# Attention scores with keys on partitions, exp without maximum behind a branch, denominators by sums and a product with ones

## The chip, the cores and the metric

The kernel runs on one core of one Trainium2 chip. A core has five engines with a queue each: TensorE for matrix products (PE in the profile, PEld for its weight loads), VectorE (DVE), ScalarE (ACT), GpSimd (POOL) and SyncE (SP, which here only issues DMAs). The matrix products here write to PSUM tiles; the other operands lie in SBUF. The metric is the device time of the whole program in microseconds (us); the median of three runs before the change is 2140.26 us (2139.71 to 2141.01).

## The reference

Attention over 8 batches, 12 heads, 448 rows and head dimension 64, with q and k divided by the root of their mean square and multiplied by g, and then a feed-forward with squared relu on the 3584 x 768 result:

```python
def rmsnorm(x, g):
    rms = np.sqrt(np.mean(x * x, axis=-1, keepdims=True) + 1e-06)
    return x / rms * g
q_n, k_n = (rmsnorm(q, g_q), rmsnorm(k, g_k))
scores = (1.0 / np.sqrt(64)) * np.matmul(q_n, k_n.transpose(0, 1, 3, 2))
scores = scores - np.max(scores, axis=-1, keepdims=True)
attn = np.exp(scores)
attn = attn / (np.sum(attn, axis=-1, keepdims=True) + 1e-09)
x = np.matmul(attn, v)         # then (B, H, S, D) -> (B*S, H*D)
h = np.maximum(x @ w_in, 0.0)  # w_in: 768 x 2048
out = h * h @ w_out            # w_out: 2048 x 768
```

The setup draws g_q and g_k as |normal| + 0.5. The weights w_in and w_out come as float64, and the kernel makes float32 numbers of their two words itself; all else is float32.

## The kernel before

A sequence of 448 rows is held as 4 chunks of 112 (NJ = 4, CP = 112): partition p holds rows 4p to 4p + 3. Heads go in pairs, 48 in all, six pairs to a batch. For a pair, `load` brings q, k and v (SP). `normalize` squares q and k (POOL, L93), sums (DVE), takes the power -1/2 (POOL, rr, L100) and multiplies q and k by it (POOL, qkn, L105). `turn` transposes both (PE, tr, L121), so that the even head's 64 dimensions lie on the lower half of the partitions and the odd head's on the upper, and multiplies by g (DVE, L122).

Then a pair has 8 steps, one for each head and chunk of queries. `score` makes 112 x 448 scores with queries on the partitions (PE, sc, L132), their negative maximum (DVE, nmax, L134), exp with the sum of each row (ACT, L137), the reciprocal of the sum and the product with it (DVE, L139 to L141). Two steps later (LAG) `turn_weights` transposes that block in four pieces (PE, trw, L150), and ACT (L153, even head) or DVE (L155, odd head) copies it out of PSUM. `attend` multiplies with v (PE, av, L165): 8 products a pair, the even head writing the lower half of the PSUM tile and the odd head the upper; one copy (DVE, L170) makes a sixth of the batch's xT.

The feed-forward of batch b - 1 is a generator, `ffn`: 16 blocks f of hps (PE, L190, six products each), relu (ACT, L199), squares on POOL (L204, L205, L209, L210), then yps (PE, L219, 16 products for each half of an output tile, 3 tiles for an even batch and 4 for an odd one), copies and stores. Its pieces are placed evenly among the steps of batch b's attention; the last batch's run alone at the end. Only PE's order is written out by hand, by this loop. The other engines' orders are made by a scheduler from priorities and its estimates, and every engine then runs its queue in order.

The weights come in 56 pieces, 24 of w_in (128 x 512) and 32 of w_out (128 x 384), over the first 72 steps (WEIGHT_STEPS), that is 9 pairs. `to_float32` needs for each piece five DVE instructions (L278, L285, L289, L293, L297), three on POOL (L282, L302, L303) and one on ACT (L301), in a chain between the engines. Pieces of w_out pass through two tiles (tag y), those of w_in through eight.

Of the kernel before, what the change touches and what calls it, by code (L numbers as in the profile page):

```python
# [10 lines left out]
F32 = mybir.dt.float32  # L11
U32 = mybir.dt.uint32
# [12 lines left out]
WEIGHT_STEPS = 72  # steps over which the weights are loaded: more than a batch's attention has  # L25
LAG = 2  # steps between a chunk's scores and the transposes of its weights
# [3 lines left out]
def kernel(  # L30
# [10 lines left out]
):  # L41
    nc = tc.nc
# [11 lines left out]
    const = ctx.enter_context(tc.tile_pool(name="const", bufs=1))  # L54
    io = ctx.enter_context(tc.tile_pool(name="io", bufs=3))
# [3 lines left out]
    ps_sc = ctx.enter_context(tc.tile_pool(name="ps_sc", bufs=3, space=bass.MemoryType.PSUM))  # L59
    ps_tr = ctx.enter_context(tc.tile_pool(name="ps_tr", bufs=2, space=bass.MemoryType.PSUM))  # L60
    ps_av = ctx.enter_context(tc.tile_pool(name="ps_av", bufs=1, space=bass.MemoryType.PSUM))
# [3 lines left out]
    gq = const.tile([P, 1], F32, name="gq")  # L65
    gk = const.tile([P, 1], F32, name="gk")
# [5 lines left out]

    pairs = [(b, c) for b in range(B) for c in range(NPAIR)]
    loaded, normal, turned, weights, xts = {}, {}, {}, {}, {}

    def load(i):
        b, c = pairs[i]
        qk = io.tile([CP, 2, 2, NJ, D], F32, name="qk", tag="qk", bufs=2)
        vt = io.tile([CP, 2, NJ, D], F32, name="vt", tag="vt")
        for dst, src in ((qk[:, 0], q), (qk[:, 1], k), (vt, v)):  # L80
            nc.sync.dma_start(
                dst.rearrange("p h j d -> p h (j d)"),
                src[b, 2 * c : 2 * c + 2].rearrange("h (p j) d -> p h (j d)", j=NJ),
            )
        loaded[i] = qk, vt

    def normalize(i):
        """Rows of q and k over their root mean square, the two heads' rows side by side."""
        qk = loaded[i][0]
        qkn = att.tile([CP, 2, NJ, 2, D], F32, name="qkn", tag="qkn", bufs=1)  # L90
        rows = qk.rearrange("p x h j d -> p (x h j) d")
        squares = qkn.rearrange("p x j h d -> p (x j h) d")
        nc.gpsimd.tensor_tensor(out=squares, in0=rows, in1=rows, op=ALU.mult)  # L93
        ms = small.tile([CP, 4 * NJ], F32, name="ms", tag="ms", bufs=2)
        nc.vector.tensor_reduce(out=ms, in_=squares, axis=AX.X, op=ALU.add)
        nc.vector.tensor_scalar(  # L96
            out=ms, in0=ms, scalar1=1.0 / D, scalar2=1e-6, op0=ALU.mult, op1=ALU.add
        )
        rr = small.tile([CP, 2, 2, NJ], F32, name="rr", tag="rr", bufs=2)
        nc.gpsimd.tensor_tensor(  # L100
            out=rr.rearrange("p x h j -> p (x h j)"), in0=ms,
            in1=minus_half.to_broadcast([CP, 4 * NJ]), op=ALU.pow,
        )
        for x in range(2):
            nc.gpsimd.tensor_tensor(  # L105
                out=qkn[:, x].rearrange("p j h d -> p h j d"),
                in0=qk[:, x],
                in1=rr[:, x, :, :, None].to_broadcast([CP, 2, NJ, D]),
                op=ALU.mult,
            )  # L110
        normal[i] = qkn

    def turn(i):
        """q and k with the head dimension on the partitions, times g (and 1/sqrt(D) for q)."""
        qkn = normal.pop(i)
        qT = att.tile([P, S], F32, name="qT", tag="qT")
        kT = att.tile([P, S], F32, name="kT", tag="kT")
        for x, (dst, g, scale) in enumerate(((qT, gq, D**-0.5), (kT, gk, 1.0))):
            tr = ps_tr.tile([P, S], F32, name="tr", tag="tr")
            for j in range(NJ):  # L120
                nc.tensor.transpose(tr[:, ts(j, CP)], qkn[:, x, j].rearrange("p h d -> p (h d)"), ident[:CP, :CP])  # L121
            nc.vector.tensor_scalar(  # L122
                out=dst, in0=tr, scalar1=g, scalar2=scale, op0=ALU.mult, op1=ALU.mult
            )
        turned[i] = qT, kT

    def score(i, e, j):
        """Attention weights of head e, for its queries of chunk j."""
        qT, kT = turned[i]
        r = ds(e * D, D)  # L130
        sc = ps_sc.tile([CP, S], F32, name="sc", tag="sc")
        nc.tensor.matmul(sc, lhsT=qT[r, ts(j, CP)], rhs=kT[r, :], start=True, stop=True)  # L132
        nmax = small.tile([CP, 1], F32, name="nmax", tag="nmax")
        nc.vector.tensor_reduce(out=nmax, in_=sc, axis=AX.X, op=ALU.max, negate=True)  # L134
        w = att.tile([CP, S], F32, name="w", tag="w", bufs=3)
        den = small.tile([CP, 1], F32, name="den", tag="den")
        nc.scalar.activation(w, sc, AF.Exp, bias=nmax, accum_out=den)  # L137
        rden = small.tile([CP, 1], F32, name="rden", tag="rden")
        nc.vector.tensor_scalar(out=den, in0=den, scalar1=1e-9, scalar2=None, op0=ALU.add)  # L139
        nc.vector.reciprocal(out=rden, in_=den)  # L140
        nc.vector.tensor_scalar(out=w, in0=w, scalar1=rden, scalar2=None, op0=ALU.mult)  # L141
        return w

    def turn_weights(i, e, j, w):
        """The weights of a chunk of queries with the keys on the partitions."""
        if (i, e) not in weights:
            weights[i, e] = att.tile([CP, NJ, S], F32, name="wT", tag="wT")
        tr = ps_tr.tile([CP, NJ, CP], F32, name="trw", tag="tr")
        for m in range(NJ):
            nc.tensor.transpose(tr[:, m, :], w[:, ts(m, CP)], ident[:CP, :CP])  # L150
        dst = weights[i, e][:, :, ts(j, CP)]
        if e == 0:
            nc.scalar.copy(dst, tr)  # L153
        else:
            nc.vector.tensor_copy(out=dst, in_=tr)  # L155

    def attend(i):
        b, c = pairs[i]
        vt = loaded.pop(i)[1]
        if c == 0:  # L160
            xts[b] = ffn_p.tile([P, NC, S], F32, name="xT", tag="xT")
        av = ps_av.tile([P, S], F32, name="av", tag="av")
        for m in range(NJ):
            for e in range(2):
                nc.tensor.matmul(  # L165
                    av[ds(e * D, D), :], lhsT=vt[:, e, m, :], rhs=weights[i, e][:, m, :],
                    start=m == 0, stop=m == NJ - 1,
                )
        del weights[i, 0], weights[i, 1], turned[i]
        nc.vector.tensor_copy(out=xts[b][:, c, :], in_=av)  # L170

# [10 lines left out]
    def ffn(b):  # L182
        """Yields after each few matrix products."""
# [3 lines left out]
        for f in range(NF):  # L187
            ps = ps_mm.tile([P, S], F32, name="hps", tag="mm")
            for c in range(NC):
                nc.tensor.matmul(  # L190
                    ps, lhsT=w_in_sb[:, c, ts(f, P)], rhs=xT[:, c, :],
# [40 lines left out]
    def store(b, tt, y):  # L232
        """The tile's rows are columns of two batches, each in runs of its chunks."""
# [10 lines left out]

    def weight_chunks():
        """Pieces of the weights in the order of their use: on chip, and in memory."""
# [8 lines left out]
    def load_weights(dst, rows, col):  # L255
# [4 lines left out]
        # In the place of tiles that the products don't need yet.  # L260
# [45 lines left out]
    for t, g in ((gq, g_q), (gk, g_k)):  # L306
        for e in range(2):
            nc.scalar.dma_start(t[ds(e * D, D), :], g.rearrange("(d one) -> d one", one=1))
    nc.vector.memset(minus_half, -0.5)
    make_identity(nc, ident)  # L310
    load(1)

    steps = 2 * NJ
    waiting = deque()
# [4 lines left out]
    with tc.manual_schedule(engines={PE}):  # L319
        normalize(0)  # L320
        turn(0)
        for i, (b, c) in enumerate(pairs):
            if i + 2 < len(pairs):
                load(i + 2)
# [60 lines left out]
```

## Time and profile before

| | before |
|---|---|
| median of 3 runs | 2140.26 us |
| span of the profiled execution | 2137.4 us |
| PE busy | 2007.0 us (94%) |
| DVE busy | 945.0 us (44%) |
| POOL busy | 646.1 us (30%) |
| ACT busy | 483.3 us (23%) |
| mean granted TensorE clock | 0.951 |

The profiled execution spans 2137.4 us from the first instruction to the last; the runs' median is 2.9 us more. Busy PE is not PE at its peak, since products are pipelined and their records overlap: the cost of a product is read from start to start. In the profile each product of float32 operands has two records, a transpose has one. A line of a group reads: line, engine, operation, out<-in, shapes, count | busy us, mean ns of one | idle time before it and what ended it.

### The profile page before, as it was taken

The numbers are of one execution on the slowest core, as the hardware profiler recorded it, in microseconds if no ns is written. First come the engines' busy times: TensorE is split into PE (matmuls) and PEld (weight loads), VectorE is DVE, ScalarE is ACT, GpSimd is POOL, SyncE is SP. The second block draws the span as 40 slices with busy tenths as digits, with TensorE's granted clock in tenths as the row PEclk, the third lists the DMA queues.
The fourth block names the chain that finished last, engine by engine and source line by source line (L and its number), as shares of the span: only waits on it lengthen the run. The fifth ranks groups of instructions, "written<-read, shape, count | busy, mean of one in ns | idle before, by whom it ended". The sixth has DMA issues, their size and how long they took to land.

```text
span 2137.4 us, 18926 instructions
## 1 busy us (share of the span) xinstructions
PE 2007.0 (94%) x6784; PEld 964.6 (45%) x6784; DVE 945.0 (44%) x2277; ACT 483.3 (23%) x1173; POOL 646.1 (30%) x622
## 2 busy tenths in 40 slices
PE   5567769999999999999999999999999999999999
PEld 2222324455445544454445544454445544455555
DVE  6888786333433344444433344344443344443000
ACT  3222332211221122212221122222222122212100
POOL 6767667211331122221231123221231113210200
PEclk9765659999999999999999999999999999999999
DMA  5311332001000100011000100001000010000000
GB/s 190 91 57 44 92 87 73 13 21 32 14 22 21 32 21 22 17 29 29 17 22 21 29 25 22 18 21 37 18 19 24 21 33 22 9 8 15 0 8 22
DMA packets 47516, 70.42 MB, mean 33 GB/s; under 512 B 4416, under 2 KB 36672, under 8 KB 47424
## 3 DMA queue, kind: packets, MB, share of 16 engines
q1 hardware_dynamic: 47104, 69.22, 11.1%
q8 instruction: 54, 0.88, 0.2%
q14 instruction: 38, 0.31, 0.0%
q10 hardware_dynamic: 320, 0.00, 0.0%
HBM read 58.20 MB, written 11.01 MB: 32 GB/s over the span
## 4 chain that ended last, share of the span: by engine, by line
PE 82%; ACT 1%; issue 0%; DMA 0%; POOL 0%; ACTq 0%
PE yps L219 27%; PE hps L190 27%; PE sc L132 14%; PE trw L150 8%; PE av L165 6%; PE tr L121 1%; ACT wT L153 1%; DMA words<-in_moe_w_out_dram 0%; POOL w_out_sb L303 0%; ACT y L228 0%; POOL words L302 0%; ACT words L301 0%; ACT h L199 0%; ACTq L228 0%; ACTq L301 0%
## 5 line engine op out<-in xcount | busy, mean ns | idle before, releaser
L190 PE MATMUL hps<-xT,w_in_sb 128*128 128x448 f32 x1536 | 609.6, 543 | 0.0
L219 PE MATMUL yps<-w_out_sb,h 128*128 128x384 f32 x1792 | 603.7, 487 | 0.0
L134 DVE TENSOR_REDUCE nmax<-sc 112x1 f32<-112x448 f32 x384 | 238.4, 621 | 660.9 <-PE sc L132 660.9
L132 PE MATMUL sc<-kT,qT 64*112 64x448 f32 x768 | 425.1, 639 | 1.5 <-DVE kT L122 1.5
L219 PEld LDWEIGHTS yps<-w_out_sb,h 128*128 128x128 f32 x1792 | 329.4, 190 | 200.0 <-issue 0.7
L137 ACT ACTIVATE w<-sc,nmax 112x448 f32<-112x448 f32 x384 | 243.9, 635 | 657.5 <-DVE nmax L134 657.3
L190 PEld LDWEIGHTS hps<-xT,w_in_sb 128*128 128x128 f32 x1536 | 281.1, 191 | 228.7 <-issue 228.7
L150 PEld LDWEIGHTS trw<-ident,w 112*112 112x112 f32 x1536 | 156.3, 141 | 348.1 <-issue 244.4
L150 PE MATMUL trw<-ident,w 112*112 112x112 f32 x1536 | 245.0, 286 | 62.3 <-DVE w L141 48.4
L93 POOL TENSOR_TENSOR qkn<-qk 112x1024 f32<-112x1024 f32 x48 | 92.2, 1920 | 519.1 <-issue 424.3
L153 ACT COPY wT<-trw 112x448 f32<-112x448 f32 x192 | 102.1, 532 | 481.8 <-PE trw L150 481.7
L141 DVE TENSOR_SCALAR w<-w,rden 112x448 f32<-112x448 f32 x384 | 204.9, 534 | 9.5
L132 PEld LDWEIGHTS sc<-kT,qT 64*112 64x112 f32 x768 | 111.6, 186 | 201.7 <-issue 193.6
L165 PE MATMUL av<-wT,vt 112*64 112x448 f32 x768 | 175.9, 592 | 22.8 <-DVE wT L155 22.5
L100 POOL TENSOR_TENSOR rr<-ms,minus_half 112x16 f32<-112x16 f32 x48 | 144.7, 3014 | 67.0 <-DVE ms L96 66.9
L209 POOL TENSOR_TENSOR h<-h 128x448 f32<-128x448 f32 x64 | 60.1, 939 | 310.0 <-ACT h L199 310.0
L204 POOL TENSOR_TENSOR h<-h 128x384 f32<-128x384 f32 x64 | 53.2, 831 | 325.8 <-ACT h L199 325.8
L199 ACT ACTIVATE h<-hps 128x448 f32<-128x448 f32 x128 | 69.4, 542 | 306.6 <-PE hps L190 306.6
L139 DVE TENSOR_SCALAR den<-den 112x1 f32<-112x1 f32 x384 | 57.7, 150 | 148.1 <-ACT w L137 148.1
L165 PEld LDWEIGHTS av<-wT,vt 112*64 112x64 f32 x768 | 56.3, 148 | 140.7 <-issue 99.1
L155 DVE COPY wT<-trw 112x448 f32<-112x448 f32 x192 | 117.8, 614 | 2.0 <-PE trw L150 1.8
L105 POOL TENSOR_TENSOR qkn<-qk,rr 112x512 f32<-112x512 f32 x96 | 99.2, 1051 | 3.8
(37 smaller groups left out, 828.5 us busy)
## 6 DMA issues: line engine op xcount, KB each, us to landing
words<-in_moe_w_in_dram SPq DMA_DIRECT2D x24, 512.0 KB, 4.1
words<-in_moe_w_out_dram SPq DMA_DIRECT2D x32, 384.0 KB, 3.1
qk<-in_q_dram SPq DMA_DIRECT2D x48, 224.0 KB, 2.9
qk<-in_k_dram SPq DMA_DIRECT2D x48, 224.0 KB, 3.1
vt<-in_v_dram SPq DMA_DIRECT2D x48, 224.0 KB, 2.7
out_dram<-y SPq DMA_DIRECT2D x8, 336.0 KB, 2.8
out_dram<-y SPq DMA_DIRECT2D x8, 288.0 KB, 2.6
out_dram<-y SPq DMA_DIRECT2D x8, 240.0 KB, 2.7
```

The costliest lines, as they stand in the source:

```text
L100: nc.gpsimd.tensor_tensor(out=rr.rearrange("p x h j -> p (x h j)"), in0=ms, in1=minus_half.to_broadcast([CP, 4 * NJ]), op=ALU.pow,)
L105: nc.gpsimd.tensor_tensor(out=qkn[:, x].rearrange("p j h d -> p h j d"), in0=qk[:, x], in1=rr[:, x, :, :, None].to_broadcast([CP, 2, NJ, D ...
L132: nc.tensor.matmul(sc, lhsT=qT[r, ts(j, CP)], rhs=kT[r, :], start=True, stop=True)
L134: nc.vector.tensor_reduce(out=nmax, in_=sc, axis=AX.X, op=ALU.max, negate=True)
L137: nc.scalar.activation(w, sc, AF.Exp, bias=nmax, accum_out=den)
L141: nc.vector.tensor_scalar(out=w, in0=w, scalar1=rden, scalar2=None, op0=ALU.mult)
L150: nc.tensor.transpose(tr[:, m, :], w[:, ts(m, CP)], ident[:CP, :CP])
L153: nc.scalar.copy(dst, tr)
L155: nc.vector.tensor_copy(out=dst, in_=tr)
L165: nc.tensor.matmul(av[ds(e * D, D), :], lhsT=vt[:, e, m, :], rhs=weights[i, e][:, m, :], start=m == 0, stop=m == NJ - 1,)
L190: nc.tensor.matmul(ps, lhsT=w_in_sb[:, c, ts(f, P)], rhs=xT[:, c, :], start=c == 0, stop=c == NC - 1,)
L219: nc.tensor.matmul(ps, lhsT=h2[f][:, ts(n, P)], rhs=w_out_sb[:, f, ts(half, HALF)], start=f == 0, stop=f == NF - 1,)
```

## The change

The kernel's body becomes a function `program`, called in two arms of a branch. Ahead of it, the elementwise product of g_q and g_k is made on one partition, and its largest magnitude compared with 7.5. Where it is at most that, every score is bounded and the arm `shift=False` runs: exp is taken without subtracting a maximum. The other arm keeps the maximum, with queries on the partitions and transposes.

In the arm without maximum:
- k is not normalized before it is transposed: `turn` transposes raw k, the product of both g's and 1/sqrt(64) goes to q alone, and 1/rms of a key becomes the scale of exp, since keys now lie on the partitions. Only q is multiplied by rr on POOL. The squares move from POOL to ACT (L131). k is loaded in two DMAs, each head's rows 64 numbers at a time, so a load has four DMAs.
- A pair has 4 steps, one for each chunk of keys. `weigh` makes the scores of both heads one behind the other (L184), with 112 keys on the partitions and 448 queries, and exp of both (ACT, L187), which already is what `attend` needs: the 32 transposes trw a pair and their copies are gone, and so are nmax, the sums of rows in exp, and the product with rden (L141).
- `add_up` adds the four chunks of a head on POOL (L201): 6 instructions of 112 x 448 a pair. A product with ones (den, L239, one for each head) sums over the partitions, and lays the result on all 64 partitions of the head. One reciprocal of 128 x 448 (DVE, L249) and one product (DVE, L253) make xT, where a copy stood.
- `attend(i - 1, n)` does one chunk in each step of pair i; den comes in step 1.
- PSUM: four banks for scores and transposes of q and k, two for av and den, two for the feed-forward (before 3, 2, 1 and 2). wT has three buffers for its two heads, xT is six tiles a batch instead of one.
- WEIGHT_STEPS is 36 of 24 a batch, so 9 pairs as before. The feed-forward of batch 0 starts at step 3 of batch 1's 24 (before at step 16 of 48), the later ones at step 4 (before step 2 of 48).

```diff
+    flag = nc.values_load(bounded, min_val=0, max_val=1)
+    with tc.If(flag > 0) as either:
+        program(tc, q, k, v, g_q, g_k, moe_w_in, moe_w_out, out, shift=False)
+    with either.Else():
+        program(tc, q, k, v, g_q, g_k, moe_w_in, moe_w_out, out, shift=True)
...
-        nc.gpsimd.tensor_tensor(out=squares, in0=rows, in1=rows, op=ALU.mult)
+            nc.scalar.activation(squares, qk[:, x], AF.Square)
...
-        for x in range(2):
             nc.gpsimd.tensor_tensor(
-                out=qkn[:, x].rearrange("p j h d -> p h j d"),
+            out=qn.rearrange("p j h d -> p h j d"),
...
+            sc = ps_sc.tile([CP, S], F32, name="sc", tag="sc")
+            nc.tensor.matmul(sc, lhsT=kT[r, ts(m, CP)], rhs=qT[r, :], start=True, stop=True)
+            scs.append(sc)
+        for e, sc in enumerate(scs):
+            nc.scalar.activation(
+                weights[i, e][:, m, :], sc, AF.Exp, scale=normal[i][2][:, 2 * m + e : 2 * m + e + 1]
             )
...
+            so_far = wT[:, 0, :] if m == 1 else sums[i, e]
+            nc.gpsimd.tensor_tensor(out=sums[i, e], in0=so_far, in1=wT[:, m, :], op=ALU.add)
...
-        nc.tensor.matmul(sc, lhsT=qT[r, ts(j, CP)], rhs=kT[r, :], start=True, stop=True)
-        nc.vector.tensor_reduce(out=nmax, in_=sc, axis=AX.X, op=ALU.max, negate=True)
-        nc.scalar.activation(w, sc, AF.Exp, bias=nmax, accum_out=den)
-        nc.vector.tensor_scalar(out=w, in0=w, scalar1=rden, scalar2=None, op0=ALU.mult)
...
+        for e in range(2):
+            nc.tensor.matmul(
+                av[ds(e * D, D), :], lhsT=vt[:, e, m, :], rhs=weights[i, e][:, m, :],
+                start=m == 0, stop=m == NJ - 1,
+            )
+        if m == 1:
+            den = ps_av.tile([P, S], F32, name="den", tag="av")
...
+                nc.vector.reciprocal(out=rden, in_=den)
...
+            nc.vector.tensor_tensor(out=xT, in0=av, in1=normal.pop(i), op=ALU.mult)
...
-                        start = LAG if b > 1 else 2 * steps
+                    start = NJ if b > 1 else WEIGHT_STEPS - NPAIR * NJ - 12
```

How the order on PE changes, in the middle of batch 1's attention, among the hps of batch 0. Before, at a step with attend (trw: transposes of weights, hps: feed-forward):

```order
L190 MATMUL hps<-xT,w_in_sb 128x448 x3
L132 MATMUL sc<-kT,qT 112x448
L165 MATMUL av<-wT,vt 64x448 x8
L150 MATMUL trw<-ident,w 112x112 x4
L190 MATMUL hps<-xT,w_in_sb 128x448 x3
```

Now, in steps 1 and 2 of a pair:

```order
L275 MATMUL hps<-xT,w_in_sb 128x448 x9
L184 MATMUL sc<-qT,kT 112x448 x2
L232 MATMUL av<-wT,vt 64x448 x2
L239 MATMUL den<-sum,ones 64x448 x2
L275 MATMUL hps<-xT,w_in_sb 128x448 x6
L184 MATMUL sc<-qT,kT 112x448 x2
L232 MATMUL av<-wT,vt 64x448 x2
L163 MATMUL tr<-ident,qn 128x112 x4
L163 MATMUL tr<-ident,qk 128x112 x4
```

The eight av of a pair are spread over its steps, both heads' sc stand together, den reads POOL's sums in PE's row, and fewer, larger groups of hps lie between.

POOL's queue, while w_out is made ready. Before, at a pair's normalization (words and w_out_sb: conversion, qkn and rr: normalization):

```order
L100 TENSOR_TENSOR rr<-ms,minus_half 112x16
L105 TENSOR_TENSOR qkn<-qk,rr 112x2x4x64 x2
L302 TENSOR_TENSOR words<-words 128x384
L303 TENSOR_TENSOR w_out_sb<-w_out_sb,words 128x384
L282 TENSOR_SCALAR w_out_sb<-w_out_sb 128x384
```

Now, among batch 0's hps, up to the last sum of pair 7:

```order
L201 TENSOR_TENSOR sum<-sum,wT 112x448
L387 TENSOR_TENSOR words<-words 128x384
L388 TENSOR_TENSOR w_out_sb<-w_out_sb,words 128x384
L367 TENSOR_SCALAR w_out_sb<-w_out_sb 128x384
L201 TENSOR_TENSOR sum<-wT 112x448
L201 TENSOR_TENSOR sum<-sum,wT 112x448
L137 TENSOR_TENSOR rr<-ms,minus_half 112x16
L201 TENSOR_TENSOR sum<-sum,wT 112x448
```

The sums, which PE's den waits for, stand in one queue with the conversion of the weights, 25 of whose 32 pieces of w_out are ahead of the last of these rows.

More of the change, by code (lines that the diff above doesn't have):

```diff
@@ L11 @@
 F32 = mybir.dt.float32
+I32 = mybir.dt.int32
 U32 = mybir.dt.uint32
@@ L144, in turn_weights @@
[L144 to L157, printed above, removed]
-        b, c = pairs[i]
[L159 to L163, printed above, removed]
+                nc.tensor.transpose(tr[:, ts(j, CP)], rows[:, j].rearrange("p h d -> p (h d)"), ident[:CP, :CP])
@@ new lines, in add_up, with weigh_shifted @@
+    def add_up(i, m):
+        if m == 0:
+            return
+        for e in range(2):
+            wT = weights[i, e]
+            if m == 1:
+                sums[i, e] = att.tile([CP, S], F32, name="sum", tag="sum", bufs=2)
+            so_far = wT[:, 0, :] if m == 1 else sums[i, e]
+            nc.gpsimd.tensor_tensor(out=sums[i, e], in0=so_far, in1=wT[:, m, :], op=ALU.add)
+    def weigh_shifted(i, m):
+        qT, kT = turned[i]
+        for e in range(2):
+            r = ds(e * D, D)
+            sc = ps_sc.tile([CP, S], F32, name="sc", tag="sc")
+            nc.tensor.matmul(sc, lhsT=qT[r, ts(m, CP)], rhs=kT[r, :], start=True, stop=True)
+            nmax = small.tile([CP, 1], F32, name="nmax", tag="nmax")
+            nc.vector.tensor_reduce(out=nmax, in_=sc, axis=AX.X, op=ALU.max, negate=True)
+            w = att.tile([CP, S], F32, name="w", tag="w", bufs=1)
+            nc.scalar.activation(w, sc, AF.Exp, bias=nmax)
+            tr = ps_sc.tile([CP, NJ, CP], F32, name="trw", tag="sc")
+            for n in range(NJ):
+                nc.tensor.transpose(tr[:, n, :], w[:, ts(n, CP)], ident[:CP, :CP])
+            nc.vector.tensor_copy(out=weights[i, e][:, :, ts(m, CP)], in_=tr)
+        if m == NJ - 1:
+            for n in range(NJ):
+                add_up(i, n)
@@ L164, in attend @@
             for e in range(2):
                 nc.tensor.matmul(
-                    av[ds(e * D, D), :], lhsT=vt[:, e, m, :], rhs=weights[i, e][:, m, :],
-                    start=m == 0, stop=m == NJ - 1,
-                )
-        del weights[i, 0], weights[i, 1], turned[i]
-        nc.vector.tensor_copy(out=xts[b][:, c, :], in_=av)
+                    den[ds(e * D, D), :], lhsT=ones, rhs=sums.pop((i, e)), start=True, stop=True
+                )
+            rden = att.tile([P, S], F32, name="rden", tag="rden", bufs=1)
@@ new lines, in attend @@
+            if shift:
+                nc.vector.tensor_scalar(
+                    out=rden, in0=den, scalar1=1e-9, scalar2=None, op0=ALU.add
+                )
+                nc.vector.reciprocal(out=rden, in_=rden)
+            else:
+                nc.vector.reciprocal(out=rden, in_=den)
+            normal[i] = rden
+        if m == NJ - 1:
+            xT = ffn_p.tile([P, S], F32, name="xT", tag="xT", bufs=NC + 2)
+            nc.vector.tensor_tensor(out=xT, in0=av, in1=normal.pop(i), op=ALU.mult)
+            xts[b][c] = xT
+            del weights[i, 0], weights[i, 1], turned[i], loaded[i], avs[i]
```

167 lines of the change are left out of this document (102 added, 65 removed).

## The prediction

> **What bounds the kernel now.** I read the page's busy rows and slices first, to find stages.
>
> ```profile
> span 2137.4 us, 18926 instructions
> PE 2007.0 (94%) x6784; PEld 964.6 (45%) x6784; DVE 945.0 (44%) x2277; ACT 483.3 (23%) x1173; POOL 646.1 (30%) x622
> ...
> PE   5567769999999999999999999999999999999999
> ...
> DVE  6888786333433344444433344344443344443000
> ...
> POOL 6767667211331122221231123221231113210200
> PEclk9765659999999999999999999999999999999999
> ```
>
> One slice is 53.4 us. There are two stages. In the first seven slices DVE and POOL are full, PE has holes and is granted 50 to 90% of its clock; afterwards PE is full at 90% or more and nothing else passes half. The windows put numbers on it (columns: time, then busy us and count of PE, PEld, DVE, ACT, POOL, then clock).
>
> ```profile
> 12.00:366.00 354.00, 252.92 (x701) 104.39 (x702) 285.79 (x647) 102.78 (x238) 250.92 (x215) 0.71 0.29 86
> 348.00:1984.00 1636.00, 1623.57 (x5706) 787.00 (x5705) 670.58 (x1655) 373.38 (x926) 391.38 (x387) 1.00 0.08 22
> ```
>
> The chain of work that ended last, asked for in order of time, starts at 342.81 us and is PE from there to the end.
>
> ```profile
> by line: PE yps L219 27.1%; PE hps L190 26.6%; PE sc L132 13.7%; PE trw L150 7.8%; PE av L165 5.9%; PE tr L121 1.1%; ACT wT L153 1.0%; issue 0.4%; DMA words<-in_moe_w_out_dram 0.1%; POOL w_out_sb L303 0.0%; ACT y L228 0.0%; POOL words L302
> ...
> 342.81 3.02 DMA words<-in_moe_w_out_dram
> 348.44 5.77 PE hps L190 x12
> ```
>
> So the second stage is a sum of PE work: products of the feed-forward, (27.1 + 26.6)% of 2137.4 = 1148 us, and attention, (13.7 + 7.8 + 5.9 + 1.1 + 1.0)% = 631 us. At 348 us, 64 steps of 8 a pair are done, so these 631 us are 40 pairs at 15.8 us. The first stage is set by DVE and POOL, which turn the weights into float32 beside the first pairs.
>
> **The change on PE, second stage.** The timeline of PE alone gives the prices (start, us, then what; each product of the program has two records).
>
> ```profile
> 20.39 3.33 PE L132 MATMUL sc<-kT,qT 64*112 64x448 f32 x6 [1.47 <-DVE kT L122]
> ...
> 27.44 1.83 PE L132 MATMUL sc<-kT,qT 64*112 64x448 f32 x2
> ...
> 1222.36 2.76 PE L219 MATMUL yps<-w_out_sb,h 128*128 128x384 f32 x8
> 1225.05 1.00 PE L132 MATMUL sc<-kT,qT 64*112 64x448 f32 x2
> 1225.98 3.23 PE L165 MATMUL av<-wT,vt 112*64 112x448 f32 x16
> 1229.14 0.60 PE L150 MATMUL trw<-ident,w 112*112 112x112 f32 x4
> 1229.58 0.82 PE L219 MATMUL yps<-w_out_sb,h 128*128 128x384 f32 x2
> ```
>
> From start to start, one head's scores hold PE for 1225.98 - 1225.05 = 0.93 us, one chunk's four transposes for 0.44, and eight products of weights and v for 3.16. In the first 30 us, where PE runs slower, one head's scores took 1.83 us and three queued together 3.33: two heads more for 1.50. The even head uses the lower row half and the odd head the upper, so two of the three ran side by side, at the price of one. The 3.16 us are eight times 0.395 for two heads each: they run side by side too.
>
> Per pair the change takes away 32 transposes (8 x 0.44 = 3.5 us) and puts the two heads' scores next to each other: 4 x 0.93 instead of 8 x 0.93, 3.7 us less. It splits weights times v into four couples, 0.79 us each, plus about 0.11 for entering (3.16 less 8 x 0.38 is 0.1), 0.90. It adds two products with ones per pair, a fifth couple beside av, 0.76. The eight transposes of q and k stay, at two chunks' price, 0.87. With 0.09 for going from yps to scores (2.69 from 1222.36 to 1225.05, less 8 x 0.325), a pair costs 4 x (0.09 + 0.93 + 0.90) + 0.76 + 0.87 = 9.3 us against 15.8.
>
> **The first stage.** Two engines share it unequally, and their durations show a coupling (lines of the first window, then of 800 to 1800 us; busy, mean ns).
>
> ```profile
> L141 DVE TENSOR_SCALAR w<-w,rden 112x448 f32<-112x448 f32 x71 | 55.0, 775 | 0.1
> L134 DVE TENSOR_REDUCE nmax<-sc 112x1 f32<-112x448 f32 x71 | 43.1, 609 | 0.8 <-PE sc L132 0.8
> ...
> L134 DVE TENSOR_REDUCE nmax<-sc 112x1 f32<-112x448 f32 x198 | 123.5, 624 | 400.8 <-PE sc L132 400.8
> L141 DVE TENSOR_SCALAR w<-w,rden 112x448 f32<-112x448 f32 x198 | 93.7, 473 | 5.9
> ```
>
> L141, SBUF to SBUF, takes 775 ns where POOL is 71% busy and 473 where it is not; L134, which reads PSUM, takes the same in both. So DVE instructions between SBUF operands wait for POOL. The change removes L141 (55 us), the maxima, the small reciprocals and the copies of transposed weights from DVE, and gives POOL the sums: the load moves to the other side of that coupling. Prices, all of the first window except the last:
>
> ```profile
> 12.00:366.00 354.00, 30.22 (x69) 14.29 (x70) 75.48 (x120) 50.86 (x48) 0.71 0.29 86
> ...
> 12.00:366.00 354.00, 0.00 (x0) 0.00 (x0) 76.45 (x160) 48.82 (x63) 0.71 0.29 86
> ...
> L302 POOL TENSOR_TENSOR words<-words 128x384 f32<-128x384 f32 (+1 forms) x55 | 68.6, 1248 | 76.1 <-issue 30.2 <-ACT wT L153 22.9 <-ACT w L137 17.7
> L100 POOL TENSOR_TENSOR rr<-ms,minus_half 112x16 f32<-112x16 f32 x11 | 37.6, 3417 | 4.0 <-DVE ms L96 3.9
> ...
> L105 POOL TENSOR_TENSOR qkn<-qk,rr 112x512 f32<-112x512 f32 x22 | 23.4, 1083 | 0.9
> ...
> L204 POOL TENSOR_TENSOR h<-h 128x384 f32<-128x384 f32 x3 | 2.5, 820 | 0.0
> L205 POOL TENSOR_TENSOR rest<-h 128x64 f32<-128x64 f32 x3 | 1.0, 327 | 0.0
> ...
> L209 POOL TENSOR_TENSOR h<-h 128x448 f32<-128x448 f32 x64 | 60.1, 939 | 310.0 <-ACT h L199 310.0
> ```
>
> The two window rows are the instructions on w_in_sb and on w_out_sb (PE, PEld, DVE, POOL): all 56 pieces of weights cost DVE 75.5 + 76.5 = 152 us and POOL 50.9 + 48.8 + 68.6 = 168.
>
> PE cannot pass the first product with ones of pair 7 before POOL has ended that pair's sums. In POOL's new order stand ahead of that point: 24 pieces of w_in and 25 of 32 of w_out (50.9 + 25/32 x 48.8 + 49/56 x 68.6 = 149 us), 11 rr (37.6), 10 qn, now of q alone (10.8), 48 sums (at L209's 0.94, the nearest two-operand row of that width: 45.1) and 7 squares of h with their rests (8.0): 250 us. DVE has 75.5 + 25/32 x 76.5 = 135 us of conversion before it, in a chain with POOL's. POOL alone is the lower bound, 250; no overlap at all is the upper, 385. Before, POOL's 251 and the 152 + 55 = 207 us of DVE's SBUF instructions fitted into 354, a ratio of 0.77; 385 x 0.77 = 298. I add 7, since POOL is now the fuller queue and each wait on it counts: 305.
>
> ```profile
> 0.73 0.38 SPq L81 DMA_DIRECT2D qk<-in_q_dram  x1
> ...
> 12.23 0.61 POOL L282 TENSOR_SCALAR w_in_sb<-w_in_sb 128x512 f32<-128x512 f32 x1 [5.80 <-DVE ms L96]
> ...
> gq<-in_g_q_dram ACTq DMA_DIRECT2D x2, 0.2 KB, 3.4
> ```
>
> The branch stands ahead of the first load, now at 0.73 us: the load of g (3.4 us), three small DVE instructions and the flag's way to five engines, which no row shows; between 4 us and 15, I take 7. POOL's first conversion then comes behind two rr and two qn, the second of which waits for qT of pair 0 on DVE; with L100 and L105 twice that is 5 to 6 us more than the 12.23 of now. POOL starts the count at 25, and den of pair 7 can run at 25 + 305 = 330 us.
>
> The Trainium skill ("SBUF — State Buffer", Who interferes with whom) says that GpSimd and VectorE share one pair of ports as an exclusive lock, held for a whole instruction, and that it is taken by VectorE's two-port copies and by its instructions with two SBUF inputs, not by reductions. The two rows of L141 and L134 agree in kind. By that rule as it stands nothing of the 385 overlaps, den of pair 7 runs at 410 and the sum below ends 80 us later; this is a rival below, reckoned from the same rows.
>
> **What lies beside.** ACT gets the squares and kT, and loses half the copies and the reading of sums: 8 x 0.63 + 2 x 0.68 + 0.53 = 7 us a pair of some 33; hidden by PE's products, and in the first stage by POOL. The reciprocal over 448 columns has no row.
>
> ```profile
> L137 ACT ACTIVATE w<-sc,nmax 112x448 f32<-112x448 f32 x71 | 44.9, 632 | 125.0 <-DVE nmax L134 124.8
> ...
> L140 DVE RECIPROCAL rden<-den 112x1 f32<-112x1 f32 x71 | 10.8, 152 | 0.1
> L139 DVE TENSOR_SCALAR den<-den 112x1 f32<-112x1 f32 x71 | 10.1, 143 | 2.9 <-ACT w L137 2.9
> L122 DVE TENSOR_SCALAR qT<-tr,gq 128x448 f32<-128x448 f32 x10 | 6.7, 674 | 3.4 <-PE tr L121 3.4
> ```
>
> Below, it is a plain instruction of that width, 0.67 us; above, each column costs what a whole one-column reciprocal does, 448 x 0.152 = 68 us. One column more than a tensor_scalar costs 9 ns, so I take 0.67 + 448 x 0.009 = 4.7 us. It has two steps, 12 us, before it is needed, and is hidden. The keys' loads in shorter runs and the fourth DMA of a load are asked for two pairs ahead, on SP, behind the weights; hidden, unless SP's wait for a free words tile passes a pair.
>
> **The sum.** When den of pair 7 can run, PE has done 10 of 16 f of the first hps, 60 of 768 products (44 us), and waits there. Left are 1148 - 44 = 1104 us of products and 39.5 pairs x 9.3 = 367. To this come waits: 8 us at den of pair 8, since POOL still has seven pieces (7/32 x 48.8 + 7/56 x 68.6 + five squares + four sums = 29 us, and part of DVE's) against 32 us of PE; 2 us at the head of each of six batches, where five steps without products (11 us of PE) meet 6 x 0.94 + 3.4 + 1.1 = 10.1 us of POOL; 5 us for the last den, reciprocal and xT: 25 us. 330 + 1104 + 367 + 25 = 1826. The profiled execution spans 2137.4 against a median of 2140.26, so 3 us lie around it: 1829, I say 1828, 14.6% less.
>
> **Rivals.**
> - POOL keeps its pace, DVE's waits hide beside it: den of pair 7 free at 275, and then PE sets the point: before hps POOL has 24 + 12 pieces, 10 rr, 9 qn and 42 sums, 197 us, so hps begin near 220, and 44 us of products with six steps of 2.4 end at 280: 1778. For it: POOL was idle 29% of the first window. Against: DVE's 775 ns.
> - The ports exclude each other wholly: 1828 + 80 = 1908. Against: 251 + 207 fitted into 354.
> - PE waits for POOL or ACT in every pair (sums behind a square that waits for relu, scores behind an unread PSUM tile), 2 us x 40: 1908. Against: PE's idle time after 348 us is 12 of 1636 us; but den is a new wait.
> - Couples do not run side by side when they stand alone: 4 x 0.93 more a pair for scores, x 40: 1977. The 3.33 us row speaks against it.
> - Slower: the reciprocal. DVE becomes the bound of the second stage once a pair costs it (2140 - 330)/40 = 45 us; its other work is about 4 us, so from 41 us, 92 ns a column, the kernel is slower; at 152 ns a column it is 330 + 40 x 72 = 3210 us. The 9 ns speak against it.
> - The flag takes the other arm, with maxima and transposes: then PE has 15.8 + 0.76 us a pair: 2140 + 30 = 2170. The reference draws |g| + 0.5 with a fixed seed; the largest product of g_q and g_k there is 5.3, under 7.5, which speaks against it.
>
> **How the numbers follow.** Forecast 0.54, own range 1790 to 1870 (first stage 300 to 360 us, pair 8.9 to 9.8). Faster first stage 0.16, strict ports 0.07, waits in every pair 0.14, no side by side 0.05, reciprocal 0.02, other arm 0.02. The range 1755 to 1900 takes in the forecast, nearly all of the first rival and the lower half of the waits, about 0.8. Runs of this kernel lie within 0.06%; 0.2% is about what can be told from no change. Faster 0.96, same 0.01, slower 0.03.
>
> **What would show it.** In the new profile: scores of two heads starting together, 0.93 us a couple; 9.3 us of attention a pair on PE; POOL over 80% busy until the last w_out piece, near 365 us; den of pair 7 near 330; the reciprocal between 0.7 and 6 us. I am wrong if PE, after the weights are in, idles over 2 us a pair, or if the first stage ends before 300 or after 370.

## The result and the profile after

| | before | after |
|---|---|---|
| median | 2139.99 us (2138.59 to 2141.01) | 1989.33 us (1988.85 to 1992.25) |
| ratio | | 0.930, interval 0.9285 to 0.9311 |
| span of the profiled execution | 2137.4 us | 1987.5 us |
| mean granted TensorE clock | 0.951 | 0.932 |

The kernel became 7.0% faster, 151 us. The forecast was 1828 us with a range of 1755 to 1900: the sign was right, the time lies 89 us above the range. The page of after, its busy rows and the slices of PE, POOL and the clock (one slice is 49.7 us):

```profile
span 1987.5 us, 14446 instructions
PE 1755.0 (88%) x5440; PEld 800.5 (40%) x5440; DVE 496.4 (25%) x602; ACT 423.6 (21%) x741; POOL 823.0 (41%) x814
PE   4446767999999999999999999999999999999998
POOL 6988877433432244423442244423442244411200
PEclk8566688999999989999999999999999999999999
```

The two stages are still there, and the first is no shorter: the chain of work that ended last reaches PE's products at 352 us, before at 348. The surprise is in the second: PE's busy share is lower than before, 88% against 94%, and the clock has a dip in a slice where before all were nines. The windows (time, busy us and count of PE, PEld, DVE, ACT, POOL, then clock, DMA share, GB/s) give the second stage as a whole and the place of a dip:

```profile
351.00:1984.00 1633.00, 1560.28 (x4936) 730.59 (x4936) 243.41 (x259) 330.65 (x575) 542.90 (x550) 0.98 0.08 23
880.00:929.00 49.00, 47.50 (x160) 24.16 (x160) 7.55 (x9) 9.22 (x16) 14.56 (x14) 1.00 0.10 28
929.50:939.00 9.50, 7.66 (x38) 2.53 (x37) 3.46 (x2) 2.91 (x5) 5.86 (x4) 1.00 0.14 41
940.00:950.00 10.00, 8.54 (x18) 2.37 (x18) 2.29 (x4) 4.62 (x8) 5.33 (x5) 0.53 0.21 61
```

PE idles 73 of 1633 us, where before it idled 12 of 1636; and around 940 us, the head of a batch, where five steps stand without products, PE is granted half its clock. No other engine is near full. The groups of PE in that window say at which lines it waits (last columns: idle time before them and what ended it):

```profile
L184 PE MATMUL sc<-qT,kT 64*112 64x448 f32 x628 | 213.0, 614 | 37.4 <-ACT wT L187 33.6 <-ACT kT L169 3.7
L232 PE MATMUL av<-wT,vt 112*64 112x448 f32 x644 | 166.4, 598 | 0.0
L239 PE MATMUL den<-sum,ones 112*64 112x448 f32 x160 | 37.4, 547 | 0.0
L163 PE MATMUL tr<-ident,qk 112*128 112x112 f32 x156 | 23.9, 277 | 37.3 <-DVE qT L165 37.3
```

den, the new wait, costs nothing. The scores wait for exp (ACT L187), and the transposes of k for DVE to read the transposes of q. The timeline of PE at the head of that batch (start, us, instruction, idle before it) shows the sequence:

```profile
934.07 1.01 PE L184 MATMUL sc<-qT,kT 64*112 64x448 f32 x4
935.01 0.97 PE L232 MATMUL av<-wT,vt 112*64 112x448 f32 x4
935.92 0.60 PE L163 MATMUL tr<-ident,qn 112*128 112x112 f32 x4
937.73 0.60 PE L163 MATMUL tr<-ident,qk 112*128 112x112 f32 x4 [1.22 <-DVE qT L165]
938.96 1.00 PE L184 MATMUL sc<-qT,kT 64*112 64x448 f32 x2 [0.62 <-ACT kT L169]
940.68 1.83 PE L184 MATMUL sc<-qT,kT 64*112 64x448 f32 x2 [0.72 <-ACT wT L187]
942.44 1.76 PE L232 MATMUL av<-wT,vt 112*64 112x448 f32 x4
944.98 2.36 PE L184 MATMUL sc<-qT,kT 64*112 64x448 f32 x4 [0.78 <-ACT wT L187]
```

A row "sc x4" is both heads' scores, two records each, side by side; "sc x2" is one head alone. At 934.07 the couple starts together, but in the last step of the pair the even head runs alone at 938.96 and the odd head at 940.68, after the even head's exp. ACT's timeline names what ACT was waiting for:

```profile
940.00 0.63 ACT L187 ACTIVATE wT<-sc,rr 112x448 f32<-112x448 f32 x1 [1.09 <-PE sc L184]
944.29 2.21 ACT L187 ACTIVATE wT<-sc,rr 112x448 f32<-112x448 f32 x4 [2.24 <-PE av L232]
```

At 944.29 four exps run in a row, released by the av of 942.44, the last of the pair before. The table of waits of after (us in total, times, longest) has this in nearly every pair:

```profile
ACT wT L187 <- PE av L232: 94.8, 45, 3.1
PE tr L163 <- DVE qT L165: 91.5, 46, 12.0
PE sc L184 <- ACT wT L187: 50.3, 60, 4.0
```

My reading, which the experiments test: wT has three tiles, each of all four chunks of one head, and a pair needs two. The even head of the next pair gets the third; the odd head's exps must wait until the last av of the pair before has read the whole tile. Until then its scores stay unread in three of the four PSUM banks. The transposes of q and k have to go through the one bank left, one behind the other, and the last couple of scores can't stand together. Of the 152 couples of sc after 400 us, 108 start within 8 ns of each other; 44 stand apart, 38 of them with the odd head at least 1.7 us behind the even one. That is about one of the four couples of a pair.

### The profile page after: what moved, and what is told of

Read it like the earlier page. It is cut to its first block, busy times and chain, and to the rows that moved or that the text cites. A ratio compares the mean times of both kernels' runs of the same rounds, so it can differ in the third digit from the quotient of the medians.

```text
span 1987.5 us, 14446 instructions
## 1 busy us (share of the span) xinstructions
PE 1755.0 (88%) x5440; PEld 800.5 (40%) x5440; DVE 496.4 (25%) x602; ACT 423.6 (21%) x741; POOL 823.0 (41%) x814
## 4 chain that ended last, share of the span: by engine, by line
PE 78%; DVE 3%; ACT 2%; POOL 0%; issue 0%; DMA 0%; ACTq 0%; POOLq 0%
PE yps L304 30%; PE hps L275 27%; PE sc L184 10%; PE av L232 8%; PE tr L163 2%; PE den L239 2%; ACT wT L187 2%; DVE qT L165 1%; DVE rden L249 1%; DMA words<-in_moe_w_out_dram 0%; POOL w_out_sb L388 0%; POOL words L387 0%; ACT kT L169 0%; DVE w_out_sb L370 0%; DVE w_out_sb L374 0%
## 5 line engine op out<-in xcount | busy, mean ns | idle before, releaser
L201 POOL TENSOR_TENSOR sum<-sum,wT 112x448 f32<-112x448 f32 x192 | 220.5, 1148 | 349.3 <-ACT wT L187 342.2
L187 ACT ACTIVATE wT<-sc,rr 112x448 f32<-112x448 f32 x384 | 227.6, 633 | 623.5 <-PE sc L184 528.5
L184 PE MATMUL sc<-qT,kT 64*112 64x448 f32 x768 | 284.6, 657 | 68.8 <-ACT wT L187 50.3
L249 DVE RECIPROCAL rden<-den 128x448 f32<-128x448 f32 x48 | 141.9, 2956 | 476.1 <-PE den L239 476.1
L201 POOL TENSOR_TENSOR sum<-wT 112x448 f32<-112x448 f32 x96 | 110.4, 1150 | 313.7 <-PE den L239 222.5
L232 PE MATMUL av<-wT,vt 112*64 112x448 f32 x768 | 209.5, 628 | 0.0
L184 PEld LDWEIGHTS sc<-qT,kT 64*112 64x112 f32 x768 | 78.8, 191 | 245.1 <-ACT wT L187 116.9
L132 DVE TENSOR_REDUCE ms<-squares 112x8 f32<-112x512 f32 x96 | 65.6, 684 | 203.8 <-ACT squares L131 194.8
L163 PE MATMUL tr<-ident,qk 112*128 112x112 f32 x192 | 32.1, 295 | 91.5 <-DVE qT L165 91.5
L131 ACT ACTIVATE squares<-qk 112x512 f32<-112x512 f32 x96 | 60.3, 628 | 104.0 <-DMA qk<-in_q_dram 49.6
L253 DVE TENSOR_TENSOR xT<-av,rden 128x448 f32<-128x448 f32 x48 | 29.9, 623 | 200.2 <-PE av L232 177.5
```

What stands on the lines that cost most here:

```text
L131: nc.scalar.activation(squares, qk[:, x], AF.Square)
L132: nc.vector.tensor_reduce(out=ms[:, ts(x, 2 * NJ)], in_=squares, axis=AX.X, op=ALU.add)
L163: nc.tensor.transpose(tr[:, ts(j, CP)], rows[:, j].rearrange("p h d -> p (h d)"), ident[:CP, :CP])
L184: nc.tensor.matmul(sc, lhsT=kT[r, ts(m, CP)], rhs=qT[r, :], start=True, stop=True)
L187: nc.scalar.activation(weights[i, e][:, m, :], sc, AF.Exp, scale=normal[i][2][:, 2 * m + e : 2 * m + e + 1])
L201: nc.gpsimd.tensor_tensor(out=sums[i, e], in0=so_far, in1=wT[:, m, :], op=ALU.add)
```

## The experiments

Each kernel was timed in three rounds beside the kernel before, whose median there was 2140.3 to 2141.4 us. Diffs are against after unless they say otherwise; "den of pair 7" is the start of that pair's product with ones, at 324 us in after.

**Chunk tiles.** wT becomes twelve tiles of one chunk instead of three of four chunks: the same bytes.

```diff
-        if m == 0:
-            for e in range(2):
-                weights[i, e] = att.tile([CP, NJ, S], F32, name="wT", tag="wT", bufs=3)
...
+        for e in range(2):
+            weights.setdefault((i, e), []).append(
+                att.tile([CP, S], F32, name="wT", tag="wT", bufs=3 * NJ)
+            )
...
-                weights[i, e][:, m, :], sc, AF.Exp, scale=normal[i][2][:, 2 * m + e : 2 * m + e + 1]
+                weights[i, e][m], sc, AF.Exp, scale=normal[i][2][:, 2 * m + e : 2 * m + e + 1]
...
```

> The exponentials go into tiles of one chunk, 12 of them, instead of 3 of four chunks: the same bytes, but a chunk's place comes free when that chunk's av has run. Buffer theory (odd head's exp waits for the last av of the former pair, holds three of four score banks full until step 3, and PE then waits for qT, kT and the even head's exp one behind the other): PE's waits for DVE qT (91.5 us on PE) and for ACT wT (50.3 us) fall under 15 us each, scores of two heads start together in every step, time 1845 to 1890 us. Bank theory (four banks are too few for two heads' scores and two transposes, however the exps go): 1970 to 1995 us. Queue theory (POOL's sums and DVE's reciprocal set the waits): within 20 us of 1989.

Measured: 1822.88 us (1822.38 to 1823.08), ratio 0.851 (0.85 to 0.8528): 166 us less than after and beyond what was expected; in this arm nothing else changes but the indices into wT. Of the 166 us 24 lie ahead of den of pair 7, at 300 instead of 324 us. The second stage and a head of a batch in the windows, the groups, what is left of the waits for exp, and that head in PE's timeline (av is L237, den L244 here):

```profile
356.00:1818.00 1462.00, 1458.71 (x4863) 701.28 (x4858) 241.73 (x258) 316.96 (x561) 527.41 (x540) 1.00 0.09 25
850.00:865.00 15.00, 15.00 (x69) 4.88 (x68) 6.31 (x7) 9.00 (x16) 8.67 (x9) 1.00 0.26 72
...
L189 PE MATMUL sc<-qT,kT 64*112 64x448 f32 x616 | 155.4, 582 | 0.0
L163 PE MATMUL tr<-ident,qk 112*128 112x112 f32 x152 | 20.8, 259 | 0.0
...
PE sc L189 <- ACT wT L192: 8.4, 3, 5.6
...
855.14 1.01 PE L189 MATMUL sc<-qT,kT 64*112 64x448 f32 x4
856.08 0.97 PE L237 MATMUL av<-wT,vt 112*64 112x448 f32 x4
856.99 0.60 PE L163 MATMUL tr<-ident,qn 112*128 112x112 f32 x4
857.42 0.55 PE L163 MATMUL tr<-ident,qk 112*128 112x112 f32 x4
857.90 1.01 PE L189 MATMUL sc<-qT,kT 64*112 64x448 f32 x4
```

PE idles 3 of 1462 us at a full clock, all 149 couples after 400 us start within 8 ns, and the table of waits has no row of the transposes of k behind qT any more. That the tiles of wT cost the time is shown.

**Eight chunk tiles.** As before this, with room for two thirds of the bytes.

```diff
-                att.tile([CP, S], F32, name="wT", tag="wT", bufs=3 * NJ)
+                att.tile([CP, S], F32, name="wT", tag="wT", bufs=2 * NJ)
```

> Exp into tiles of one chunk, but eight of them, two thirds of the bytes of the three whole tiles. If it is when a buffer comes free that counts (a chunk is given back after its own product, not after all four), the time stays near that with twelve chunk tiles, 1823 to 1850. If it was the amount of room, it is slower than with three whole tiles or at least near them: 1960 or more.

Measured: 1823.37 us (1823.11 to 1824.1), the same as with twelve. What counts is when a buffer is given back, not how much room there is.

**Before, with the heads together.** One part of the change put alone into the kernel before.

```diff
+    scores = {}
...
     def score(i, e, j):
...
-        qT, kT = turned[i]
-        r = ds(e * D, D)
-        sc = ps_sc.tile([CP, S], F32, name="sc", tag="sc")
-        nc.tensor.matmul(sc, lhsT=qT[r, ts(j, CP)], rhs=kT[r, :], start=True, stop=True)
+        if e == 0:
+            qT, kT = turned[i]
+            for x in range(2):
+                r = ds(x * D, D)
+                scores[x] = ps_sc.tile([CP, S], F32, name="sc", tag="sc")
+                nc.tensor.matmul(
+                    scores[x], lhsT=qT[r, ts(j, CP)], rhs=kT[r, :], start=True, stop=True
+                )
+        sc = scores[e]
```

> The kernel before with one part of the change alone: the scores of both heads of a pair are issued next to each other on the two row halves; max, exp and the transposes of the probabilities stay. If couples on the halves run side by side wherever they stand together, up to 40 pairs x 4.1 us come off: 1976 to 2020, less what the banks of the scores and the max on VectorE make wait. If they don't, or if the scores wait for banks that VectorE and ScalarE have not read, 2120 to 2145.

Measured: 2011.55 us (2010.37 to 2011.92), ratio 0.940 (0.9382 to 0.9413): 129 us less than before by the order of instructions alone. PE's groups from 351 to 1990 us, first of before, then of this kernel:

```profile
L132 PE MATMUL sc<-kT,qT 64*112 64x448 f32 x630 | 315.8, 582 | 0.0
L121 PE MATMUL tr<-ident,qkn 112*128 112x112 f32 x304 | 42.7, 263 | 12.2 <-ACT wT L153 12.2
```

```profile
L136 PE MATMUL sc<-kT,qT 64*112 64x448 f32 x628 | 162.2, 582 | 0.0
L121 PE MATMUL tr<-ident,qkn 112*128 112x112 f32 x308 | 43.7, 265 | 49.6 <-ACT wT L160 49.6
```

One product lasts 582 ns in both, but the scores hold PE for half the time: 154 us less, of which 37 come back where the transposes of q and k wait for ACT to copy transposed weights out of PSUM. The Trainium skill ("TensorE: Matmul & The Clock Gate", Part 3) says that products on different row groups of the array overlap, starting about 4 ns apart; here the rows agree on the overlap, for float32 and halves of 64 rows, and with chunk tiles the two heads' records start 6 to 7 ns apart.

**No branch.** The arm without maximum is called directly; the test of g and the other arm are left out.

```diff
...
-    with tc.If(flag > 0) as either:
-        program(tc, q, k, v, g_q, g_k, moe_w_in, moe_w_out, out, shift=False)
-    with either.Else():
-        program(tc, q, k, v, g_q, g_k, moe_w_in, moe_w_out, out, shift=True)
+    program(tc, q, k, v, g_q, g_k, moe_w_in, moe_w_out, out, shift=False)
```

> The flag and the branch are left out, and the arm without maximum runs by itself. If the branch costs what its chain at the start shows (load of g, three small DVE instructions, flag to five engines), 1989 less 5 to 10 us; if code of two arms costs more than that, over 20 us less; all theories of the second stage expect the rest unchanged.

Measured: 1986.71 us (1984.61 to 1990.2), 2.6 us less than after, with ranges that overlap, and less than the 5 to 10 expected. POOL's timeline is clearer: the first conversion of weights starts 3.1 us earlier than in after. First after, then this kernel:

```profile
21.87 0.61 POOL L367 TENSOR_SCALAR w_in_sb<-w_in_sb 128x512 f32<-128x512 f32 x1
```

```profile
18.77 0.61 POOL L348 TENSOR_SCALAR w_in_sb<-w_in_sb 128x512 f32<-128x512 f32 x1
```

**A copy for the reciprocal.** The division by the denominators is left out of the result.

```diff
-                nc.vector.reciprocal(out=rden, in_=den)
+                nc.vector.tensor_copy(out=rden, in_=den)
```

> The reciprocal of the denominators (2.96 us each) is a plain copy, so the division is left out of the result. Buffer theory: only DVE's queue gets shorter, 10 to 30 us less, from the first stage and the heads of the batches. Queue theory: 60 us less or more, since rden stands between den and xT and qT behind it.

Measured: 1992.8 us (1987.53 to 1995.42), ratio 0.930 (0.9284 to 0.9315), no different from after. The two instructions in the groups of after and of this kernel:

```profile
L249 DVE RECIPROCAL rden<-den 128x448 f32<-128x448 f32 x48 | 141.9, 2956 | 476.1 <-PE den L239 476.1
```

```profile
L249 DVE COPY rden<-den 128x448 f32<-128x448 f32 x48 | 29.9, 623 | 484.4 <-PE den L239 484.4
```

2.33 us an instruction less, 48 times, moved nothing. PE's wait at the transposes of k for qT, which stands behind the reciprocal on DVE, is 89.7 us here against 91.5 in after, so it is not the reciprocal's doing. The theory of a late DVE queue falls, and so do the 10 to 30 us that I expected by my own.

**First sums on PE.** For pairs 0 to 8 POOL's sums are left out, and den is four products with ones a head, added up in PSUM.

```diff
-        add_up(i, m)
+        if not (i < 9):
+            add_up(i, m)
...
+            for n in range(NJ if (i < 9) and not shift else 0):
+                for e in range(2):
+                    nc.tensor.matmul(
+                        den[ds(e * D, D), :], lhsT=ones, rhs=weights[i, e][:, n, :], start=n == 0, stop=n == NJ - 1
+                    )
```

> For the first 9 pairs, while the weights are made ready, PE sums the four chunks itself by four products with ones a head instead of one, and POOL makes no sums (54 of 1.15 us fewer). If POOL sets the first stage: den of pair 7 near 265 to 285 us instead of 324, time 1930 to 1960. If the chain between DVE, POOL and the DMAs of w_out through two tiles sets it: den of pair 7 within 15 us of 324, time over 1970. The second stage stays.

Measured: 1960.79 us (1959.93 to 1962.84), 28.5 less than after; den of pair 7 at 309 us, the last piece of w_out ready at 315 instead of 352. The time is just past the range of the first expectation, and that den at the edge of the second's, so neither is borne out whole. The 54 sums took 66.5 us of POOL in after, so a microsecond taken from POOL there was worth a little under half. Against it stand PE's added products with ones: den holds PE for 23.0 us ahead of that point, in after for 11.1.

**Chunk tiles and first sums on PE.** Both edits together.

> The chunk tiles together with the sums of the first nine pairs on TensorE (no POOL sums). If the two causes add, the 28 to 40 us that the sums on TensorE gave with whole tiles come off the 1823 us of the chunk tiles: 1783 to 1795. If the POOL sums only mattered because they lengthened the wait for whole tiles, the gain is gone here: 1815 to 1830.

Measured: 1792.37 us (1791.22 to 1793.06), ratio 0.837 (0.8359 to 0.8387). The 30.5 us come off as before, so the two causes add. It is faster than either alone, 197 us less than after.

**More tiles for w_out.** The kernel just told, with the first 18 pieces of w_out in the eight tiles that w_in has left.

```diff
-        tag, bufs = ("h2", NF // 2) if n == DFF // 4 else ("y", 2)
+        tag, bufs = ("h2", NF // 2) if n == DFF // 4 or n_chunks - len(chunks) <= 42 else ("y", 2)
```

> As the kernel with chunk tiles and sums on TensorE, with the first 18 pieces of w_out passing through the eight tiles of h2 instead of two of y. If the conversions of weights hold up the first stage because only two tiles take the loads, the first stage shortens by a further 20 to 40 us and the time is 1750 to 1775. If the first stage is then TensorE's own, the same as the kernel before it in this list, within 5 us.

Measured: 1791.25 us (1790.19 to 1791.62) against 1792.37: the two tiles don't set the first stage, though the last piece of w_out is ready at 288 instead of 308 us.

**No limit on the weights** and **no power of two**: the chunk tiles, less one POOL instruction for each piece of weights, or one of DVE.

```diff
-        nc.gpsimd.tensor_scalar(
-            out=dst, in0=dst, scalar1=MOST, scalar2=FEW, op0=ALU.min, op1=ALU.max
-        )
```

> The kernel with chunk tiles, without POOL's limiting instruction (min and max) on each piece of weights; in this run the limiting of weights to the range of float32 is left out. Ahead of the first product with ones of pair 7 that is 18.3 + 25/32 x 17.3 = 32 us of POOL. If POOL's queue alone sets the first stage, that product comes 32 us earlier (268 instead of 300) and the time is near 1791. If POOL's and DVE's work add up at the 0.77 of the prediction, 24 us: 1799. If the first stage hangs on something else (the loads, PE's own work and clock), under 8 us: 1815 to 1823.

```diff
-        nc.vector.tensor_scalar(
-            out=high, in0=bits, scalar1=0x40000000, scalar2=0xFF800000,
-            op0=ALU.bitwise_xor, op1=ALU.bitwise_and,
-        )
```

> The kernel with chunk tiles, without the DVE instruction that takes the power of two out of each piece of weights; the low words are then scaled by a wrong factor, so the last bits of the weights differ. Ahead of the first product with ones of pair 7 that is 14.0 + 25/32 x 13.3 = 24 us of DVE. If POOL's queue alone sets the first stage, no change: 1818 to 1825. If POOL's and DVE's work add up at the 0.77 of the prediction, 19 us: 1804.

Measured: 1805.07 us (1803.68 to 1805.87) without POOL's instruction, 17.8 less than with chunk tiles; 1822.09 (1821.05 to 1823.9) without DVE's, no change. Den of pair 7 starts at 284 and at 300 us, against 300. No expectation fits both: in the first stage these 24 us of DVE are hidden, and POOL's come through by about half. With chunk tiles only 21 pieces of w_out, not 25, stand ahead of that den, which makes 29.8 us of limiting. Without it POOL was busy for 228 us from 12 us to that den, 19 less than the 247 with chunk tiles: its 48 sums took 66.5 us instead of 60.1, and two more pieces of w_out stood ahead. Why the sums grew these runs don't settle. Without DVE's instruction the last piece of w_out is ready at 339 instead of 360 us, and the time stays.

## Why the prediction was wrong

What follows sums, for each line, the time from each product's start on PE to the next product's start, from den of pair 7 to the end. A wait between two products thus stands at the first of them.

| from den of pair 7 | predicted | after | chunk tiles |
|---|---|---|---|
| den of pair 7 | 330 | 324 | 300 |
| products | 1104 | 1135 | 1152 |
| attention, 39.5 pairs | 367 (9.3 a pair) | 522 (13.2) | 363 (9.2) |
| waits listed apart; measured: after the last product | 25 | 6 | 6 |

- **The step that failed** is "To this come waits: ... 25 us". It lists waits at den and at the heads of batches and holds none for a tile of wT that is given back late: the attention took 522 us instead of 367, 155 more. The change's own list had it in words, "wT has three buffers for its two heads", and I costed attention from start to start of instructions without asking when each one's tile is given back. Against after, the chunk tiles save 159 us of attention (89 at sc, 51 at tr and 20 at av in the booking above). In after, 41 us of PE's idle time end at sc and 42 at tr; the rest is scores that run alone and the half clock.
- **The rival was right in kind.** "PE waits for POOL or ACT in every pair", with scores behind an unread bank, had 0.14 and 2 us a pair. It was 13.2 - 9.3 = 3.9 us a pair, twice the price; and the argument against it, that PE idled 12 of 1636 us before, came from a kernel in which exp wrote one step's scores to a tile of their own, not to a part of a tile that four chunks share. The sign that I had named for it, PE idle for over 2 us a pair, did not even show: the 73 us of idle time are about 1.9 a pair, and the rest of the loss lies in records that count as busy.
- **The prices of the attention were right.** With chunk tiles a pair costs 9.2 us against 9.3, waits and all: the couple of scores 0.94 (855.14 to 856.08) against 0.93, av 0.91 (856.08 to 856.99) against 0.90, the transposes 0.91 (856.99 to 857.90) against 0.87. That couples run side by side is shown by the kernel before with heads together; that rival is out.
- **Products** were low by 31 us: I took 1148 us from the shares of the chain, which book the passage from a product to an attention step at the step, while I priced the steps from start to start. From start to start the products of before sum to 1176 us after 348 us, 28 more. The 1152 with chunk tiles hold 13 us of waits for relu ahead of den of pair 8.
- **The first stage came out right by luck.** 330 us was to be POOL's last sum of pair 7, with PE waiting. The sum ended at 319.8, but PE came later still and didn't wait for it (POOL, PE and ACT of after, then PE's share of the stretch in after and with chunk tiles):

```profile
318.66 1.12 POOL L201 TENSOR_TENSOR sum<-sum,wT 112x448 f32<-112x448 f32 x1
```

```profile
293.32 1.01 PE L163 MATMUL tr<-ident,qn 112*128 112x112 f32 x4 [10.20 <-ACT wT L187]
298.11 1.01 PE L163 MATMUL tr<-ident,qk 112*128 112x112 f32 x4 [3.79 <-DVE qT L165]
...
323.26 0.97 PE L232 MATMUL av<-wT,vt 112*64 112x448 f32 x4
324.06 0.92 PE L239 MATMUL den<-sum,ones 112*64 112x448 f32 x4
```

```profile
292.20 0.55 ACT L386 ACTIVATE words<-words 128x384 f32<-128x384 uint32 x1 [7.44 <-DMA words<-in_moe_w_out_dram]
292.65 0.61 ACT L187 ACTIVATE wT<-sc,rr 112x448 f32<-112x448 f32 x1
```

```profile
25.00:324.00 299.00, 175.06 (x447) 61.36 (x448) 226.07 (x297) 76.86 (x139) 251.98 (x230) 0.69 0.29 85
```

```profile
25.00:300.00 275.00, 150.07 (x450) 55.45 (x450) 201.80 (x270) 72.88 (x133) 238.07 (x213) 0.73 0.30 85
```

  The 10.20 us are not the wait for a whole tile: the exp stood in ACT's queue behind a conversion that waited 7.44 us for its weights to be loaded. I had counted ACT as hidden. The chunk tiles bring den to 300 us, though PE idles as long ahead of it (125 us against 124); it is busy for 25 us less over nearly the same number of records, 19 of them at sc, whose heads stand together more often. The ratio of 0.77 on the sum of POOL's and DVE's work was wrong in form: taking 24 us from DVE changed nothing, taking 30 from POOL brought 18. Strict exclusion by the ports, as I read the rule of the Trainium skill ("SBUF — State Buffer", Who interferes with whom) for all of DVE's work, put den of pair 7 at 410 and is out; a DVE instruction taken away would have counted in full.
- **Small terms.** The branch was 3.1 us against 7. The reciprocal was 2.96 us against 4.7 and hidden, as forecast. A POOL sum of two different tiles was 1.24 us in the first stage (1.13 later) against the 0.94 of a square, 15 us more over 48 sums. Den of pair 8 came at 380 us against 370; there the conversion of weights on DVE's queue delayed qT and rden, which ran at 343 us for the den of 324.
- The chunk-tile kernel's 1823 us lies 5 us from the forecast, but that too is partly luck: its first stage is 30 us shorter than in the forecast's sum and what follows 25 us longer.

## What to carry to other kernels

When a change makes a step shorter or groups instructions, list for each tile who reads it last and when it comes free, and follow the wait backward: here an exp that had no tile kept PSUM banks full, and those stopped transposes and couples in the next steps. A buffer of several chunks is given back only after its last chunk is read; the same bytes in tiles of one chunk were worth 166 us, more than the whole change had been. An idle share of the kernel before is no evidence on a wait whose buffers the change rearranges, and an idle share of the kernel after misses what the wait costs in records that count as busy.

## What the hardware showed that I had not expected

Short waits cost more than their length here, since the clock went down with them. In the head of a batch PE was busy 8.54 of 10 us and was granted 0.53 of its clock from 940 to 950 us, just after 1.00 up to 939 us (shown above); the odd head's scores took 1.83 us there against the even head's 1.00. With chunk tiles a head of a batch runs without a hole and at the full clock (15.00 of 15 us busy at 1.00, from 850 to 865 us). The Trainium skill ("TensorE: Matmul & The Clock Gate", Part 1) says that the gate passes half the pulses or all, depending on how busy the array has lately been; the nearly doubled durations agree with the two values. What length of idle time triggers it no run here isolates.
